# A planner that writes each engine's order: one plan in program order, against 25 plans ranked by latest starts

## The chip, the cores and the metric

The kernel runs on one core of a Trainium2 chip. A core has five engines that run their own instruction streams and meet only at semaphores: PE (TensorE, matrix products; its weight loads appear as PEld), DVE (VectorE), ACT (ScalarE), POOL (GpSimd) and SP (SyncE, which issues nearly all DMA transfers here). The metric is the device time of one execution in microseconds; less is better. All arithmetic is in 32-bit floats.

## The reference

The sequence has 2048 positions and 512 channels. Two layers alternate, A, B, A, B, each on a layer norm of x and added to x:

```python
L = 2 * S                                            # layer A
kv = k_shift * v                                     # k_shift: 4 taps, causal, per channel
y = irfft2(rfft2(pad(kv)) * rfft2(pad(ssm_k)))[:S]   # long convolution per channel
y = y + kv * ssm_D
A = q * y                                            # q = layernorm(x)

P = exp((A * dt)[:, :, None] * pos)                  # layer B: 128 modes per channel
K = 2.0 * einsum("dn,dnl->dl", C, P).real            # its convolution kernel, 512 x 2048
B = irfft(rfft(K) * rfft(u))[:L] + u * D_skip        # u = layernorm(x)
```

A's y does not depend on x, and B's K does not either, so each is computed once and used twice.

## The kernel before

The Fourier transforms are products with constant matrices on PE (w1, w2 forward, mm and w4 back). The channels are worked in four quarters of 128, each quarter in four groups of 32, and the frequencies in eight chunks.

The work has two parts, and the planner orders each as a whole.

Part 1 (2211 operations) holds two streams and the start of a third.

- The K stream makes B's kernel in 64 taps, four to each of 16 groups. A tap is: PE computes angles (pa, from tt and rw) and subtracts the whole turns (y on DVE, then pa<-y,minus on PE), ACT takes Abs and five Sin, POOL and DVE multiply by the magnitudes m (xy, and e on DVE), and PE contracts (pk<-xy,e; the number behind e names the tap). The magnitudes are Exp on ACT, for two groups at a time. After a group DVE writes ks, SP stores it (kdram) and loads it back (kk), PE and DVE transform it (pf<-kk, zk, pf<-zk), ACT copies the spectrum (pc) and SP stores it (spec). Exp and Sin need different ACT tables, and ordering edges in the program keep the Exp and Sin phases apart.
- The A stream forms kv (prod on POOL, kv<-prod,minus on PE, prod on DVE, stored in kv_d), the spectrum of ssm_k (through kk and zk as well), and then convolves quarter by quarter: u loaded from kv_d, pf<-u, transposes zu, pf<-zu, products vv and sw with the loaded spectrum kab on DVE, pf<-vv and pf<-sw, ACT copies zu, DVE transposes w, PE forms kv<-w, ACT copies and SP stores ya, and DVE updates the tile xq of the residual (two operations, kv<-kv,rs and xq<-kv,xq). When a quarter's four groups are done, SP stores xq in x1_d (shown as x_d), and xq, which has one buffer, is loaded for the next quarter; POOL subtracts a mean first.
- The start of the first B layer: x is loaded from x_d, a normalizer makes its scale rs and offset nb, and u, pf<-u and zu follow.

Part 2 (824 operations) is the first B convolution (pu<-zu, copies sw on ACT, products vv on DVE and sw on POOL, pi<-vv and pi<-sw, copies ie, transposes w, po<-w, x<-x,po, statistics st<-x), then the second A layer (`gated_update`: x is multiplied row block by row block by ut, made from the stored ya), a normalizer for each half of the rows, and the second B convolution, which ends in yo and its stores. Before the second convolution adds to x, `restore` on DVE adds the mean off back to each of 16 row blocks (x<-x,off). A restore of a row block has to follow the operations u that read the block.

Who sets the order: the helper `Planner` records every operation (`record`), and at `flush` it makes a plan and emits the instructions of each engine in the plan's order, with edges that keep this order. `cost` gives each operation how long it holds its engine and when its result is there. `plan` is a list scheduler in time: among the operations whose producers are planned it takes, again and again, the one that could begin earliest; where several could begin at the same time on an engine, the smaller rank goes first. The buffers that an operation needs have to be free, DMAs share eight lanes, large two-input products on DVE and POOL exclude each other, and the PE clock is taken as half after a little used window of 3413 ns. Before, rank is the place in the program, and there is one plan (`best`):

```python
    def best(self):
        return self.plan()
```

All instructions of the planned parts are issued from one line, 411 before and 485 in the changed kernel, so they are told apart by tiles. Line 178 (179) issues the prelude, which is not planned. In the profile pf stands for several PSUM tiles that share a pool.

Of the kernel before, what the change touches and what calls it, by code (L numbers as in the profile page):

```python
# [18 lines left out]
L, D, NM = 2048, 512, 128  # L19
# [88 lines left out]

class Planner:
    FIFO = False  # L110
    RELEASE = {"V": 34, "S": 60, "G": 90, "T": 80, "D": 27}

    def __init__(self, tc, nc):
# [107 lines left out]
    def prepare(self):  # L221
        ops = self.ops
        self.costs = [self.cost(op) for op in ops]
        for op in ops:
            op.before = {o for o in op.before if ops[o.n:o.n + 1] == [o]}
            op.ordered = [o for o in op.ordered if ops[o.n:o.n + 1] == [o]]
            op.late = [(o, lead) for o, lead in op.late if ops[o.n:o.n + 1] == [o]]
        self.follow = [[] for _ in ops]
        for op in ops:
            for o in op.before:  # L230
                self.follow[o.n].append((op.n, True))
            for o in op.ordered:
                self.follow[o.n].append((op.n, False))
            for o, lead in op.late:
                self.follow[o.n].append((op.n, lead))
        self.pending = [len(op.before) + len(op.ordered) + len(op.late) for op in ops]
        names, self.prior, self.queue = {}, [], {}
        self.using, self.users, self.gate, self.tag, self.handles, self.buffers = [], [], [], [], [], {}
        self.held = {p: [] for p in self.over.values()}
        for op in ops:  # L240
            l = []
            for t in op.uses:
                if t.tag_meta is None:
                    continue
                if t.name not in names:
                    names[t.name] = len(self.prior)
                    pool = next((p for p in self.over if f"_{p}_" in t.tag), None)
                    self.gate.append(self.over.get(pool))
                    q = self.queue.setdefault(t.tag, [])
                    ring = self.name(t) not in self.shared  # L250
                    self.prior.append(q[-t.tag_meta.bufs] if ring and len(q) >= t.tag_meta.bufs else None)
                    self.tag.append(None if ring else t.tag)
                    self.handles.append(t)
                    q.append(len(self.prior) - 1)
                    if not ring and len(q) <= t.tag_meta.bufs:
                        self.buffers.setdefault(t.tag, []).append(t)
                    self.users.append(0)
                l.append(names[t.name])
                self.users[names[t.name]] += 1
            self.using.append(l)  # L260
            for p, h in self.held.items():
                if any(f"_{p}_" in t.tag for t in op.uses if t.tag_meta is not None):
                    h.append(op.n)

    def plan(self, rank=None):
        ops, costs, prior, using = self.ops, self.costs, self.prior, self.using
        rank = rank or list(range(len(ops)))
        pending, left = list(self.pending), list(self.users)
        idle, live = [0.0] * len(prior), [False] * len(prior)
# [8 lines left out]
        ready = [0.0] * len(ops)  # L278
        start, end = [0.0] * len(ops), [0.0] * len(ops)
        avail = {e: [] for e in self.engines}  # L280
        lanes, server, lock = [0.0] * 8, 0.0, {"V": 0.0, "G": 0.0}
        act, window, clock = {}, 0, 0.5
        for op in ops:
            if not pending[op.n]:
                avail[op.engine].append(op.n)
        for waiting in range(len(ops)):
            best = None
            for e, l in avail.items():
                pick = None
                base = free[e]  # L290
                if e == "D":
                    base = max(base, min(lanes))
                for n in l:
                    t = max(base, ready[n])
                    if e in "VG" and costs[n][2]:
                        t = max(t, lock["G" if e == "V" else "V"])
                    if pick is not None and (t, rank[n]) >= pick[:2]:
                        continue
                    ok = True
                    for u in using[n]:  # L300
                        if live[u]:
                            continue
                        if self.gate[u]:
                            if rest[self.gate[u]]:
                                ok = False
                                break
                            t = max(t, last[self.gate[u]] + self.RELEASE[e])
                        tag = self.tag[u]
                        if tag:
                            if not open_[tag] or (self.FIFO and self.queue[tag][head[tag]] != u):  # L310
                                ok = False
                                break
                            t = max(t, min(spare[tag][b] for b in open_[tag]) + self.RELEASE[e])
                            continue
                        if prior[u] is None:
                            continue
                        if left[prior[u]]:
                            ok = False
                            break
                        t = max(t, idle[prior[u]] + self.RELEASE[e])  # L320
                    if not ok:
                        continue
                    if pick is None or (t, rank[n]) < pick[:2]:
                        pick = (t, rank[n], n)
                if pick is not None and (best is None or pick[0] < best[0]):
                    best = (pick[0], pick[2], e)
            if best is None:
                return None
            t, n, e = best
            op = ops[n]  # L330
            avail[e].remove(n)
            for u in using[n]:
                tag = self.tag[u]
                if tag and not live[u]:
                    fit = [b for b in open_[tag] if spare[tag][b] + self.RELEASE[e] <= t + 1e-6]
                    self.place[u] = max(fit, key=lambda b: (spare[tag][b], -b))
                    open_[tag].remove(self.place[u])
                    head[tag] += 1
                live[u] = True
            o, lat, extra = costs[n]  # L340
            start[n] = t
            if e == "T":
                k = int(t / 3413)
# [3 lines left out]
                o = o / clock  # L347
                a = extra * o / max(costs[n][0], 1e-9) * clock / 1.0
# [26 lines left out]
            for f, real in self.follow[n]:  # L375
                pending[f] -= 1
                ready[f] = max(ready[f], end[n] + self.RELEASE[ops[f].engine] if real is True else start[n] + o if real is False else end[n] - real)
                if not pending[f]:
                    avail[ops[f].engine].append(f)
        self.length = max(end)  # L380
        return sorted(range(len(ops)), key=lambda n: (start[n], n))

    def best(self):
        return self.plan()

    @staticmethod
    def name(t):
# [913 lines left out]
```

## Time and profile before

| | us |
|---|---|
| runs | 715.59, 710.18, 705.59 |
| median of the runs | 710.18 |
| the profiled execution | 708.18 |
| its span, first to last instruction | 706.2 |

The profiled execution is 2.0 us under the median and 2.0 us over its own span. A page of the profile gives busy time per engine; a view by windows gives the same for stretches of the span, with the TensorE clock that was granted there (1.00 is full speed); the chain of waits follows the work that ended last back from the end; a timeline lists instructions with the idle time ahead of them and what ended it. PE busy time is modelled from pipelined matmuls, so a busy PE is not PE at its peak.

### The profile page before, as it was taken

What the parts mean: (1) busy time and instruction counts of PE and PEld (TensorE: products, weight loads), DVE (VectorE), ACT (ScalarE), POOL (GpSimd) and SP (SyncE); (2) the same over time, 40 slices, a digit from 0 to 9 for tenths busy, and PEclk for the clock granted to TensorE, in tenths of its full rate; (3) what the DMA queues carried; (4) which work ended last, traced back from release to release, by engine and by line L of the source; (5) the groups of instructions that cost most, each with busy time, mean ns of one, the idle gap of its engine ahead of it and who ended that gap; (6) DMA issues with size and microseconds to landing.
All of it is one profiled execution on the core that took longest, in us unless ns stands there. A gap on an engine that the chain in (4) does not pass through costs nothing. (4 is left out here: it accounts for less than half of the span.)

```text
span 706.2 us, 20796 instructions
## 1 busy us (share of the span) xinstructions
PE 536.0 (76%) x8568; PEld 297.8 (42%) x8568; DVE 473.4 (67%) x900; ACT 405.4 (57%) x768; POOL 352.7 (50%) x344
## 2 busy tenths in 40 slices
PE   1398789899888876888887894527997832789984
PEld 0124334344344344554453562213664601356652
DVE  7345653456436571878899597555678889798783
ACT  3238566857597768776265763446653418837441
POOL 3739958969777362622252644103543510255561
PEclk9999998999998696999899898759999965999998
DMA  9699996876655253555786655786766421057884
GB/s 250 211 231 254 304 228 181 223 204 204 232 168 180 82 175 104 178 184 160 224 277 217 188 167 165 253 268 220 265 248 241 153 90 59 2 185 252 297 259 89
DMA packets 74499, 138.95 MB, mean 197 GB/s; under 512 B 8093, under 2 KB 37157, under 8 KB 72357
## 3 DMA queue, kind: packets, MB, share of 16 engines
q1 hardware_dynamic: 73540, 135.21, 63.1%
q0 software_dynamic: 864, 2.43, 1.0%
q8 instruction: 67, 1.10, 0.7%
q14 instruction: 28, 0.22, 0.1%
HBM read 97.75 MB, written 39.85 MB: 195 GB/s over the span
## 5 line engine op out<-in xcount | busy, mean ns | idle before, releaser
L411 POOL TENSOR_TENSOR xy<-tt,m 128x512 f32<-128x512 f32 x128 | 148.3, 1184 | 128.4 <-issue 73.6
L411 POOL TENSOR_TENSOR sw<-sw,kab 128x512 f32<-128x512 f32 x64 | 81.2, 1292 | 116.5 <-ACT sw L411 105.0
L411 POOL TENSOR_TENSOR prod<-kvt 128x512 f32<-128x512 f32 x64 | 79.9, 1274 | 7.5 <-DVE st L411 4.9
L411 PE MATMUL pf<-u,w 64*128 64x512 f32 (+1 forms) x200 | 60.1, 693 | 28.6 <-ACT u L411 15.9
L411 PE MATMUL kv<-prod,minus 128*128 128x512 f32 x128 | 75.9, 684 | 2.9 <-POOL prod L411 2.0
L411 DVE TENSOR_TENSOR e<-pa,m 128x512 f32<-128x512 f32 x64 | 43.4, 680 | 46.5 <-ACT pa L411 42.5
L411 PE MATMUL pf<-kk,w 64*128 64x512 f32 x128 | 45.7, 757 | 38.0 <-DMA kk<-ssmk_in 13.7
L411 ACT ACTIVATE m<-pf 128x1024 f32<-128x1024 f32 x48 | 47.7, 1024 | 44.0 <-PE pf L411 42.5
L411 DVE STREAM_TRANSPOSE zu<-pf 128x512 f32<-128x512 f32 x96 | 63.2, 692 | 12.4 <-PE pf L411 12.4
L411 DVE TENSOR_SCALAR y<-pa 128x512 fp32r<-128x512 f32 x64 | 43.5, 681 | 31.2 <-PE pa L411 29.2
L411 DVE STREAM_TRANSPOSE zk<-pf 128x512 f32<-128x512 f32 x64 | 42.0, 692 | 31.7 <-PE pf L411 31.7
L411 ACT ACTIVATE ab<-pa 128x512 f32<-128x512 f32 x64 | 38.2, 597 | 42.1 <-PE pa L411 42.0
L411 ACT COPY ie<-pi 128x1024 f32<-128x1024 f32 x32 | 32.3, 1010 | 52.1 <-PE pi L411 52.1
L411 DVE TENSOR_TENSOR vv<-pu,kab 128x512 f32<-128x512 f32 x64 | 42.8, 678 | 24.6 <-ACT sw L411 20.0
L411 PE MATMUL pi<-vv,mm 64*64 64x128 f32 x1024 | 53.7, 277 | 3.4 <-DVE vv L411 2.6
L411 PE MATMUL pi<-sw,mm 64*64 64x128 f32 x1024 | 52.4, 272 | 0.0
L411 ACT COPY sw<-pu 128x1024 f32<-128x1024 f32 x32 | 32.3, 1012 | 31.8 <-PE pu L411 22.4
L411 PE MATMUL pk<-xy,e 128*32 128x64 f32 x2048 | 45.7, 234 | 5.1 <-POOL xy L411 3.6
L411 ACT COPY pc<-pf 128x512 f32<-128x512 f32 x64 | 35.6, 585 | 22.9 <-DMA spec<-pc 13.8
L411 PEld LDWEIGHTS pk<-xy,e 128*32 128x32 f32 x2048 | 34.7, 117 | 31.7 <-issue 16.7
L411 PE MATMUL po<-w,w 128*64 128x512 f32 x128 | 36.8, 675 | 11.6 <-DVE w L411 11.5
L411 ACT ACTIVATE u<-x,nb,rs 128x128 f32<-128x128 f32 x101 | 40.8, 482 | 6.4 <-DMA x<-x_d 5.3
(121 smaller groups left out, 1083.9 us busy)
## 6 DMA issues: line engine op xcount, KB each, us to landing
kab<-spec SPq DMA_DIRECT2D x94, 512.0 KB, 4.8
spec<-pc SPq DMA_DIRECT2D x64, 256.0 KB, 3.4
kvt<-kv_in SPq DMA_DIRECT2D x32, 312.0 KB, 4.8
kk<-ssmk_in SPq DMA_DIRECT2D x32, 128.0 KB, 4.9
xr<-x_in SPq DMA_DIRECT2D x8, 512.0 KB, 8.6
kv_d<-prod SPq DMA_DIRECT2D x16, 256.0 KB, 3.3
kdram<-ks SPq DMA_DIRECT2D x64, 64.0 KB, 1.8
kk<-kdram SPq DMA_DIRECT2D x32, 128.0 KB, 2.6
```

The lines of the kernel that those rows point to most:

```text
L411: ins = getattr(self.engines[op.engine], name)(*a, **k).ins
```

## The change

The planner now plans 25 times for each part and keeps the shortest plan.

- The first plan has program order as its rank, as before, but amended costs: an activation whose table is not the loaded one begins `SWAP` = 1290 ns after its engine is free, and an operation that has to wait for more than one other engine pays `EXTRA` per further engine (37 ns on DVE, 60 on ACT, 54 on POOL, 90 on PE).
- `latest` goes back through a plan from its end: over data edges, over the order in which buffers were handed on, and gives each operation the latest start that would not lengthen the plan.
- In 24 turns the rank is made from these latest starts of the turn before (turns 0, 3, 6, ...: the latest start alone; 1, 4, ...: latest plus actual start; 2, 5, ...: the place in order of the latest starts plus the place in the program).
- A new condition, `need`, keeps an operation from taking a shared buffer while an unshared buffer that its user needs is not free yet, so that a plan with other ranks cannot lock itself.

In part 1 the order of turn 3 is kept, in part 2 that of turn 6; both rank by the latest start alone. The instructions are the same in kind and number on every engine, and there are 21 ACT_TABLE_LOAD before and after.

```diff
+    SWAP, EXTRA = 1290, {"V": 37, "S": 60, "G": 54, "T": 90, "D": 0}
...
+        groups = {"Sin": "Sin", "Exp": "Exp", "Sqrt": "Sqrt", "Ln": "Ln", "Arctan": "Arctan"}
+        self.table = [groups.get(getattr(op.calls[0][1][2], "name", None)) if op.calls[0][0] == "activation" else None
+                      for op in ops]
+        self.sources = [[o.n for o in op.before] for op in ops]
...
+        self.need = [set() for _ in self.prior]
+        for l in self.using:
+            for u in l:
+                if self.tag[u]:
+                    self.need[u].update(w for w in l if not self.tag[w])
+        self.need = [{w for w in s if self.prior[w] is not None and self.prior[w] not in s} for s in self.need]
...
-                    t = max(base, ready[n])
+                    t = max(base + (self.SWAP if self.table[n] not in (None, table) else 0), ready[n])
...
+                            if any(not live[w] and left[prior[w]] for w in self.need[u]):
+                                ok = False
+                                break
...
+            table = self.table[n] or table
+            waits = set()
+            for m in self.sources[n]:
+                if ops[m].engine != e and start[m] > seen.get((e, ops[m].engine), -1.0):
+                    waits.add(ops[m].engine)
...
+            t += self.EXTRA[e] * max(0, len(waits) - 1)
...
+    def latest(self):
...
+        late = [0.0] * len(ops)
+        for a in sorted(range(len(ops)), key=lambda n: (-start[n], -n)):
+            late[a] = min([late[f] - lag for f, lag in after[a]], default=self.length) if after[a] else self.length
+            late[a] = min(late[a], self.length - (end[a] - start[a]))
+        return late
+
+    TURNS = 24
+
     def best(self):
-        return self.plan()
+        order = self.plan()
+        best = self.length, order, self.place, self.starts, self.ends
+        for turn in range(self.TURNS):
+            late, early = self.latest(), self.starts
+            if turn % 3 == 2:
+                place = sorted(range(len(late)), key=lambda n: late[n])
+                rank = [0.0] * len(late)
+                for i, n in enumerate(place):
+                    rank[n] = i + n
+            else:
+                rank = [l + (e if turn % 3 else l) for l, e in zip(late, early)]
+            order = self.plan(rank)
+            if order is None:
+                break
+            if self.length < best[0]:
+                best = self.length, order, self.place, self.starts, self.ends
+        self.length, order, self.place, self.starts, self.ends = best
+        return order
```

Three places where instructions stand otherwise are shown with the prediction's steps.

More of the change, by code (lines that the diff above doesn't have):

```diff
@@ L282, in plan @@
         act, window, clock = {}, 0, 0.5
+        table, seen = None, {}
         for op in ops:
@@ L340, in plan @@
             o, lat, extra = costs[n]
+            table = self.table[n] or table
[3 more added lines that the diff above has]
+                    waits.add(ops[m].engine)
+            for m in self.sources[n]:
+                key = e, ops[m].engine
+                seen[key] = max(seen.get(key, -1.0), start[m])
+            t += self.EXTRA[e] * max(0, len(waits) - 1)
             start[n] = t
@@ L379, in plan @@
                     avail[ops[f].engine].append(f)
-        self.length = max(end)
+        self.length, self.starts, self.ends = max(end), start, end
         return sorted(range(len(ops)), key=lambda n: (start[n], n))
-    def best(self):
-        return self.plan()
+    def latest(self):
+        ops, start, end = self.ops, self.starts, self.ends
+        after = [[] for _ in ops]
+        for a in range(len(ops)):
+            for f, real in self.follow[a]:
+                lag = end[a] - start[a] + self.RELEASE[ops[f].engine] if real is True else (
+                    self.costs[a][0] if real is False else end[a] - start[a] - real)
+                after[a].append((f, lag))
+        first, users, chains, pairs = {}, {}, {}, []
+        for a in sorted(range(len(ops)), key=lambda n: start[n]):
+            for u in self.using[a]:
+                first.setdefault(u, a)
+                users.setdefault(u, []).append(a)
+        for u in first:
+            if self.tag[u]:
+                chain = chains.setdefault((self.tag[u], self.place[u]), [])
+                if chain:
+                    pairs.append((chain[-1], u))
+                chain.append(u)
+            elif self.prior[u] in users:
+                pairs.append((self.prior[u], u))
+        for p, u in pairs:
+            for a in users[p]:
+                after[a].append((first[u], end[a] - start[a] + self.RELEASE[ops[first[u]].engine]))
+        late = [0.0] * len(ops)
[3 more added lines that the diff above has]
+        return late
```

## The prediction

> **What bounds the kernel now.** I read the page's busy times, then a view by windows cut where the kind of work changes, then the chain of waits and timelines of the stretches in which no engine is full. First the page: PE is busiest, at 76%, so no engine bounds the whole.
>
> ```profile
> span 706.2 us, 20796 instructions
> PE 536.0 (76%) x8568; PEld 297.8 (42%) x8568; DVE 473.4 (67%) x900; ACT 405.4 (57%) x768; POOL 352.7 (50%) x344
> ```
>
> The windows are: the start; K taps beside A's kv; K taps beside A's convolution; end of part 1 and x's reload; first B convolution; second gated update; last B convolution.
>
> ```profile
> core 0: us, PE busy (x) PEld busy (x) DVE busy (x) ACT busy (x) POOL busy (x), PEclk, DMA share, GB/s
> 0.00:44.00 44.00, 16.03 (x28) 4.43 (x28) 23.00 (x36) 11.36 (x17) 21.41 (x35) 0.96 0.86 229
> 44.00:220.00 176.00, 156.79 (x1869) 74.00 (x1869) 90.03 (x158) 121.14 (x252) 143.27 (x136) 0.96 0.79 222
> 220.00:425.00 205.00, 168.12 (x3070) 101.50 (x3068) 150.93 (x263) 137.97 (x271) 86.70 (x84) 0.88 0.58 177
> 425.00:480.00 55.00, 24.93 (x300) 11.30 (x302) 34.53 (x97) 24.97 (x57) 10.13 (x11) 0.72 0.75 236
> 480.00:560.00 80.00, 67.19 (x1496) 44.90 (x1491) 59.66 (x108) 39.91 (x57) 40.22 (x32) 0.98 0.66 234
> 560.00:620.00 60.00, 30.46 (x288) 14.32 (x278) 50.68 (x151) 32.72 (x70) 9.84 (x15) 0.74 0.13 45
> 620.00:706.20 86.20, 72.52 (x1549) 47.35 (x1544) 64.60 (x90) 37.37 (x48) 41.17 (x33) 0.95 0.71 222
> ```
>
> Both B convolutions keep PE at .84. The second row has PE at .89 and POOL at .81 while DVE has half its time free; the third has PE at .82 with a clock of .88, DVE at .74 and POOL at .42. So in the bulk the mix is uneven, and the fourth and sixth rows are chains in which PE is half idle. There is the time that an order can move.
>
> **The change, part by part.** It adds and removes no instruction; all its price is in order. The first tap of A's convolution on PE:
>
> ```profile
> L411 PE MATMUL pf<-u,w x200: 376/664/1219, 220.3 to 666.4; 64*128 64x512 f32 x92, 64*128 64x256 f32 x8
> ```
>
> On PE, where A's convolution begins (pf<-u), before; pk<-xy,e ends a K tap:
>
> ```order
> L411 MATMUL pk<-xy,e_622 32x64 x16
> L411 MATMUL pa<-y,minus 128x512
> L411 MATMUL pf<-kk,w_107 128x16x16x2 x2
> L411 MATMUL pa<-y,minus 128x512
> L411 MATMUL pf<-kk,w_107 128x16x16x2 x2
> L411 MATMUL pa<-tt,rw 128x512
> L411 MATMUL pf<-u,w_107 128x16x16x2 x2
> ```
>
> The same place on PE in the changed kernel:
>
> ```order
> L485 MATMUL pk<-xy,e_574 32x64 x16
> L485 MATMUL kv<-prod,minus 128x512
> L485 MATMUL pf<-zk,w_108 64x128 x16
> L485 MATMUL kv<-prod,minus 128x512
> L485 MATMUL pa<-y,minus 128x512
> L485 MATMUL pf<-u,w_107 128x16x16x2 x2
> ```
>
> The convolution moved from behind tap 29 (e_622) to behind tap 24 (e_574), and it runs beside kv products that POOL feeds.
>
> *Bulk, 44 to 425.* DVE-heavy work enters a stage where DVE is half free, and POOL-heavy taps are left for the stage where POOL has 58% free. PE's share over both stages is (156.79+168.12)/381 = .853. If the evener mix brings the second stage to that share it lasts 168.12/.853 = 197.1 instead of 205: **−7.9, taken**. Best end: it reaches the first stage's .891, 188.7, −16.3. Worst end: the more interleaved work leaves longer gaps, as in the slice 240 to 280, with 30.30/40 = .757: 222.1, +17.1. I take −7.9 as the value between the two measured stages, the nearest rows of such a mix.
>
> ```profile
> 160.00:200.00 40.00, 35.96 (x429) 16.95 (x429) 19.64 (x31) 25.81 (x51) 32.84 (x31) 1.00 0.65 205
> 240.00:280.00 40.00, 30.30 (x520) 18.90 (x524) 21.43 (x38) 28.99 (x61) 18.19 (x20) 0.76 0.46 140
> ```
>
> At the head SP issues the first rw loads behind 21 other transfers instead of 9, and POOL's kv products start later, but PE has the spectrum work (pf<-kk, pf<-zk) in their place; I cost that at nothing, and if that cover fails it falls within the range above.
>
> *End of part 1.* Of the windows' fourth row, 425.22 to 457.56 lies between the stores of the third and fourth residual quarter (x_d<-xq), 32.3 us. The chain:
>
> ```profile
> 425.22 0.34 SPq L411 DMA_DIRECT2D x_d<-xq  x1
> 429.76 1.25 SPq L411 DMA_DIRECT2D xq<-x_in  x2
> 433.36 2.13 SPq L411 DMA_DIRECT2D xq<-x_in  x2
> 436.89 1.79 SPq L411 DMA_DIRECT2D kdram<-ks  x4
> 438.96 4.03 POOL L411 TENSOR_TENSOR xq<-xq,off 128x512 f32<-128x512 f32 x4 [4.88 <-DMA xq<-x_in]
> 440.17 1.19 SPq L411 DMA_DIRECT2D kk<-kdram  x2
> 443.03 0.69 DVE L411 SCALAR_TENSOR_TENSOR xq<-kv,xq 128x512 f32<-128x512 f32 x1 [5.64 <-POOL xq L411]
> 443.69 2.16 PE L411 MATMUL pf<-kk,w 64*128 64x512 f32 x4 [8.18 <-DMA kk<-kdram]
> 445.78 1.97 PE L411 MATMUL kv<-w,w 128*64 128x512 f32 x4
> 445.89 1.31 DVE L411 STREAM_TRANSPOSE zk<-pf 128x512 f32<-128x512 f32 x2 [2.17 <-PE pf L411]
> 447.68 2.34 PE L411 MATMUL pf<-zk,w 64*64 64x128 f32 x64
> 450.51 1.08 PE L411 MATMUL kv<-w,w 128*64 128x512 f32 x4 [0.48 <-DVE xq L411]
> 457.56 0.32 SPq L411 DMA_DIRECT2D x_d<-xq  x1
> 440.77 2.78 DMA kk<-kdram
> ```
>
> The last K taps still run after the store; their kernel goes through kdram, and A's second kv<-w stands behind pf<-kk on PE, which waits 8.18 for the load. On PE the end of part 1, before:
>
> ```order
> L411 MATMUL pk<-xy,e_1082 32x64 x16
> L411 MATMUL pf<-kk,w_107 128x16x16x2 x2
> L411 MATMUL pk<-xy,e_1093 32x64 x16
> L411 MATMUL pf<-kk,w_107 128x16x16x2 x2
> L411 MATMUL kv<-w,w_110 64x512 x2
> L411 MATMUL pf<-zk,w_108 64x128 x32
> L411 MATMUL kv<-w,w_110 64x512 x2
> L411 MATMUL pf<-zk,w_108 64x128 x32
> L411 MATMUL kv<-w,w_110 64x512 x2
> ```
>
> And in the changed kernel:
>
> ```order
> L485 MATMUL pf<-vv,mm 64x128 x4
> L485 MATMUL pf<-sw,mm 64x128 x4
> L485 MATMUL pf<-kk,w_107 128x16x16x2 x2
> L485 MATMUL kv<-w,w_110 64x512 x2
> L485 MATMUL pf<-kk,w_107 128x16x16x2 x2
> L485 MATMUL pf<-zk,w_108 64x128 x64
> L485 MATMUL kv<-w,w_110 64x512 x6
> ```
>
> All taps (e_1093 is the last) now stand ahead of A's last products, and the whole transform of the last kernel ahead of kv<-w of the groups 1 to 3. On SP, kdram is issued behind the third store and ahead of xq's loads, kk's last pair between the two pairs of xq. Counting from the store: the first pair of xq can go at +4.5 as before (429.76−425.22), kk's pair 1.19 and the second xq pair 1.25 behind it, so +8.2; landed 438.96−433.36−2.13 = 3.5 later, +11.7; POOL's four subtractions 4.03, +15.8 (before +17.8). The K side: kk issued by +7.0, landed 2.78 later, +9.8; pf<-kk 2.16, zk 1.31, and 64 pf<-zk twice 2.34: +18.0. Then come kv<-w of the groups 1 to 3; the first of them before stood at 445.78−425.22 = 20.6. So −2.5, and the pf<-zk that stood between two kv<-w are gone and the first kv<-w runs at 1.08 instead of 1.97, −0.9: **−3.4**. Ends: 0, if SP's loads are as late as before, and −4.8, if K's side is entirely covered (15.8 against 20.6).
>
> *Second gated update.* DVE is 84% busy from 560 to 620, and here its order counts:
>
> ```profile
> 603.78 0.17 DVE L411 TENSOR_TENSOR nb<-nm,rs 128x8 f32<-128x8 f32 x1
> 603.98 1.70 DVE L411 TENSOR_SCALAR u<-x,rs,nb 128x128 f32<-128x128 f32 x6
> 605.73 1.99 PE L411 MATMUL pf<-u,w 64*128 64x256 f32 x12 [0.36 <-POOL u L411]
> 608.35 1.73 DVE L411 TENSOR_SCALAR x<-x,off 128x512 f32<-128x512 f32 x4 [2.67 <-ACT u L411]
> 610.00 4.90 DVE L411 STREAM_TRANSPOSE zu<-pf 128x512 f32<-128x512 f32 x8
> 611.46 3.27 PE L411 MATMUL pf<-u,w 64*128 64x512 f32 x8 [3.74 <-DVE zu L411]
> ```
>
> DVE waits 2.67 for ACT's u to restore x (x<-x,off), and the transposes zu, for which PE then waits 3.74, are queued behind that. On DVE at this place, before:
>
> ```order
> L411 TENSOR_SCALAR u<-x,rs,nb 128x128 x6
> L411 TENSOR_SCALAR x<-x,off 128x512 x4
> L411 STREAM_TRANSPOSE zu<-pf 128x512 x8
> L411 TENSOR_SCALAR x<-x,off 128x512
> L411 STREAM_TRANSPOSE zu<-pf 128x512 x2
> ```
>
> And in the changed kernel:
>
> ```order
> L485 TENSOR_SCALAR u<-x,rs,nb 128x128 x6
> L485 TENSOR_TENSOR nb<-nm,rs 128x8
> L485 TENSOR_SCALAR u<-x,rs,nb 128x128 x5
> L485 STREAM_TRANSPOSE zu<-pf 128x512 x10
> L485 TENSOR_SCALAR x<-x,off 128x512
> ```
>
> The restores moved behind the transposes, into the last convolution, where DVE is .75 and PE .84 busy and which therefore covers them. But five more u stand on DVE, since the first half's normalizer and u now come only behind the last rows. Five u of 1.70/6 = .28 are 1.4, so zu can begin about 1.4 behind the 605.7 at which u ends, near 607.0 instead of 610.0: **−3.0**. Ends: 0, if the late first half makes PE's first pf<-u as late as the restores made zu, and −4.3, if zu comes at 605.7.
>
> *The rest.* In the first B convolution some statistics move behind transposes of w, with PE at .84 as the bound; last tail unchanged: 0, ±2.
>
> ACT's table loads are now charged. Their price in the trace:
>
> ```profile
> L411 ACT ACT_TABLE_LOAD x17 | 21.8, 1283 | 6.0 <-DVE zk L411 3.6 <-DVE zu L411 2.2
> 389.78 1.03 ACT m L411
> 390.83 1.28 ACT L411
> 392.12 1.05 ACT tt L411 x3
> ```
>
> One load takes 1.28, and Sin starts right behind it; the planner's 1290 is that. The Trainium skill, ScalarE: Activation LUTs, section What ACT_TABLE_LOAD costs, adds a drain of about 1.38 us to each load; by that page the plan would still be 17 × 1.38 = 23 us of ACT time short (an estimate), but these rows show no such drain.
>
> **Sum.** 708.2 − 7.9 − 3.4 − 3.0 = 693.9, so **694.0**. The profiled execution is 2.0 under the median of 710.18, and the runs spread by ±5.
>
> **Rivals.**
> 1. *The bulk gives nothing.* Its gaps come from chains across engines, not from the mix; for it speaks that POOL's .81 in the first stage already leaves PE .89. Then 708.2 − 3.4 − 3.0 = 701.8. That the ranks do nothing of what they say is ruled out by the listings, except in the bulk, where it is this case.
> 2. *The interleaving thins PE and the clock falls.* For it: a slice that mixes both streams already ran with PE at .757 and a clock of .76, while the slice 160 to 200, with .90, had 1.00. If the second stage falls to .757, the bulk costs 17.1 and the time is 718.9; 725.3 if both tails also give nothing. It decides below a PE share of 168.12/(205+6.4) = .795, where the tails' gains are used up. Against it: even in the sixth window, with PE at 30.46/60 = .51, the clock was still .74, and DVE, ACT and POOL have room in both stages. The Trainium skill, TensorE: Matmul & The Clock Gate, section What's actually happening, says that the clock goes to half after an idle window of some 3.4 us, so longer single gaps would cost more than their length; the two slices agree in direction, and by that rule this rival would be somewhat dearer than its price here.
> 3. *The mix evens out wholly.* The second stage reaches .891: 708.2 − 16.3 − 6.4 = 685.5. Against it: DVE at .74 would have to go to .80 on average.
>
> **Chances.** The forecast's case (687 to 699) .45, rival 1 .20, rival 2 .15, rival 3 .17, others .03. A measurement of this kernel can tell about 2% from no change: 696.0 and 724.4. Faster: two thirds of the forecast's case and rival 3, with a little of the others, .49. Slower: those of rival 2 with the tails lost and some of the others, .09. Same: .42. The range goes from 680.0 (708.2 − 16.3 − 4.8 − 4.3 − 2 = 680.8) to 722.0, between rival 2's two times; a tenth is left out above, some hundredths below.
>
> **What would show it.** Bulk: the first pf<-u clearly ahead of 220, and from 44 to the third x_d<-xq less than 381 with PE's share above .853 and a clock above .88. End of part 1: the third to the fourth x_d<-xq under 32.3, and kv<-w of groups 1 to 3 in one row, not behind a wait for kk. Update: no restore between u and zu on DVE, zu some 3 from the last nb (6.2 before). Wrong if: pf<-u is early but POOL's taps then run out late; the last xq loads are stuck on SP behind spectrum stores; or zu waits for PE.

## The result and the profile after

| | before | changed |
|---|---|---|
| median of the runs, us | 709.21 (4 runs, 705.59 to 715.59) | 679.54 (4 runs, 674.84 to 683.90) |
| the profiled execution | 708.18 | 683.90 |
| its span | 706.2 | 681.4 |

The ratio is 0.9571, with a 95% interval from 0.947 to 0.9673: faster by 3.3 to 5.3%. The forecast of 694.0 had the direction; the time lies just under its range. The changed kernel's profiled execution is 4.4 over its median, so the stretches below add up to 24.8 us, less than the 29.7 between the medians.

The page of the changed kernel, its first lines:

```profile
span 681.4 us, 20786 instructions
PE 529.9 (78%) x8568; PEld 294.5 (43%) x8568; DVE 474.3 (70%) x900; ACT 407.0 (60%) x768; POOL 353.1 (52%) x344
```

Work is the same; PE, DVE and ACT have it packed closer. The view by windows of the changed kernel, cut at events: first transforms; to the third store x_d<-xq; to the fourth; to the first pu of the first B convolution; to the first ut; to the last convolution's first pu; end.

```profile
core 0: us, PE busy (x) PEld busy (x) DVE busy (x) ACT busy (x) POOL busy (x), PEclk, DMA share, GB/s
0.00:39.50 39.50, 9.89 (x20) 2.90 (x20) 21.58 (x35) 11.36 (x17) 12.79 (x27) 1.00 0.80 218
39.50:403.83 364.33, 326.64 (x4888) 171.65 (x4892) 245.63 (x424) 263.96 (x530) 242.03 (x229) 0.94 0.73 210
403.83:446.30 42.47, 21.59 (x320) 11.62 (x312) 19.95 (x40) 10.52 (x17) 7.49 (x10) 0.74 0.59 165
446.30:467.20 20.90, 5.73 (x16) 1.82 (x17) 13.64 (x55) 10.62 (x28) 0.00 (x0) 0.61 0.89 271
467.20:563.80 96.60, 74.73 (x1648) 49.54 (x1648) 77.69 (x172) 44.15 (x66) 43.15 (x35) 0.97 0.62 216
563.80:591.66 27.86, 15.61 (x44) 7.60 (x45) 25.80 (x74) 25.46 (x59) 4.36 (x10) 0.73 0.11 38
591.66:681.40 89.74, 75.71 (x1644) 49.35 (x1644) 69.98 (x102) 40.91 (x55) 43.30 (x34) 0.96 0.68 213
```

The same cut of the kernel before, for the bulk and for the first B convolution:

```profile
44.00:425.22 381.22, 325.14 (x4940) 175.57 (x4944) 241.18 (x422) 259.33 (x521) 229.97 (x219) 0.91 0.68 198
479.20:583.47 104.27, 79.24 (x1648) 50.43 (x1648) 78.28 (x172) 44.12 (x65) 42.98 (x35) 0.93 0.56 198
```

In the bulk PE was idle for 381.2 − 325.1 = 56.1 us and is so for 37.7 now; its share went from .853 to .897. Cut once more at the first pf<-u (220.3 and 200.5), it went from .89 to .92 ahead of A's convolution and from .82 to .88 beside it. PE's three longest waits in the bulk before, each ended by work of the K stream (m, e, y), and the same three now, by the view of waits (us in total, times, longest):

```profile
PE pf L411 <- ACT m L411: 10.1, 10, 1.9
PE pa L411 <- DVE e L411: 8.7, 12, 2.9
PE pa L411 <- DVE y L411: 5.3, 10, 1.4
```

```profile
PE pf L485 <- ACT m L485: 5.7, 11, 1.5
PE pa L485 <- DVE e L485: 5.7, 10, 1.1
PE pa L485 <- DVE y L485: 2.4, 4, 0.8
```

Not all waits shrank: PE's wait for the products vv of A rose from 1.6 to 5.2. From the start times of the same events in both traces (nb is the last one on DVE):

| stretch | before | changed | difference | forecast |
|---|---|---|---|---|
| start to third x_d store | 425.22 | 403.83 | −21.4 | −7.9 |
| third to fourth x_d store | 32.34 | 42.47 | +10.1 | −3.4 |
| to the first pu | 21.60 | 20.90 | −0.7 | 0 |
| first pu to first ut (first B convolution) | 104.30 | 96.56 | −7.7 | 0 |
| first ut to last nb | 20.31 | 19.74 | −0.6 | 0 |
| last nb to first pu of the last convolution | 11.26 | 8.15 | −3.1 | −3.0 |
| from there to the end | 91.19 | 89.74 | −1.4 | 0 |

Three terms are off: the bulk gained more than twice what was said, the end of part 1 lost instead of gaining, and the first B convolution gained where nothing was expected.

### The profile page after: what moved, and what is told of

Its sections match the earlier page's. It is cut to its first block, busy times and chain, and to the rows that moved or that the text cites. A ratio compares the mean times of both kernels' runs of the same rounds, so it can differ in the third digit from the quotient of the medians.

```text
span 681.4 us, 20786 instructions
## 1 busy us (share of the span) xinstructions
PE 529.9 (78%) x8568; PEld 294.5 (43%) x8568; DVE 474.3 (70%) x900; ACT 407.0 (60%) x768; POOL 353.1 (52%) x344
## 5 line engine op out<-in xcount | busy, mean ns | idle before, releaser
L485 PE MATMUL pf<-u,w 64*128 64x512 f32 (+1 forms) x200 | 56.8, 659 | 22.8 <-ACT u L485 19.2
L485 ACT COPY pc<-pf 128x512 f32<-128x512 f32 x64 | 35.4, 588 | 59.8 <-PE pf L485 42.0
L485 ACT COPY ie<-pi 128x1024 f32<-128x1024 f32 x32 | 32.3, 1009 | 49.2 <-PE pi L485 49.2
L485 ACT ACTIVATE m<-pf 128x1024 f32<-128x1024 f32 x48 | 47.1, 1027 | 16.3 <-PE pf L485 15.2
L485 ACT COPY sw<-pu 128x1024 f32<-128x1024 f32 x32 | 32.1, 1012 | 24.2 <-PE pu L485 13.6
L485 PE MATMUL pf<-zk,w 64*64 64x128 f32 x1024 | 39.0, 295 | 6.4 <-DVE zk L485 4.6
```

What stands on the lines that cost most here:

```text
L485: ins = getattr(self.engines[op.engine], name)(*a, **k).ins
```

## The experiments

Each was timed beside the kernel before on the same chip; the medians of the kernel before lay between 710.0 and 711.5 there. The times are medians, the ratio is to the kernel before.

| run | us | ratio (95%) |
|---|---|---|
| e1_costs_only | 696.83 | 0.9789 (0.9738 to 0.9839) |
| e2_turns_only | 708.36 | 0.9940 (0.9900 to 0.9979) |
| e3_part1_new | 693.00 | 0.9722 (0.9655 to 0.9788) |
| e4_part2_new | 695.99 | 0.9786 (0.9726 to 0.9846) |
| e5_ya_first | 672.40 | 0.9475 (0.9417 to 0.9534) |
| e6_shift_only | 720.11 | 1.0164 (1.0092 to 1.0237) |
| e7_swap_only | 691.00 | 0.9734 (0.9662 to 0.9806) |
| e8_swap_2660 | 686.15 | 0.9669 (0.9603 to 0.9736) |
| e9_stats_late | 702.10 | 0.9799 (0.9718 to 0.9880) |
| e10_restore_late | 709.11 | 0.9953 (0.9915 to 0.9990) |
| e11_charges_low | 675.43 | 0.9460 (0.9378 to 0.9542) |
| e12_charges_high | 679.42 | 0.9519 (0.9454 to 0.9583) |
| e13_random_ranks | 700.12 | 0.9887 (0.9833 to 0.9941) |
| e14_first_turn | 696.28 | 0.9781 (0.9702 to 0.9860) |

**Charges and turns apart.**

```diff
-    TURNS = 24
+    TURNS = 0
```

> The changed planner with no turns: one plan in program order, with the charges for table loads and second waits. Its order begins A's convolution behind the same tap as the changed kernel (e_574, before e_622). Theory (the early start evens the mix in the bulk): nearly the whole bulk gain of 17 to 21 us stays and the time is 685 to 693. Rival (the ranking by latest start makes the gain, the charges do nothing alone): within 4 us of the kernel before, 705 to 713.

```diff
-    SWAP, EXTRA = 1290, {"V": 37, "S": 60, "G": 54, "T": 90, "D": 0}
+    SWAP, EXTRA = 0, {"V": 0, "S": 0, "G": 0, "T": 0, "D": 0}
```

> 24 turns with ranks from latest starts, but no charge for table loads and none for second waits. A's convolution begins behind e_545, earlier still. Theory (early start): the bulk gain stays, 677 to 690. Rival (the charges are what makes the plan fit the chip): the plan misjudges ACT and the time is 700 to 712.

For the charges neither theory holds whole; for the turns alone the rival came. The charges alone give 13.5 us (710.4 to 696.8), the turns alone 2.0, both together 29.7: one needs the other. PE's idle time from the start to the third x_d store says the same: 84.1 us before, 75.2 with the charges alone, 86.2 with the turns alone, 67.3 with both. Charges alone begin A's convolution at 194.3, earlier than the changed kernel (200.5), and yet reach the third x_d store only at 414.4. The reason why the turns alone bring so little is in ACT's groups, of e2:

```profile
L485 ACT ACT_TABLE_LOAD x27 | 34.6, 1283 | 0.5
L485 ACT ACTIVATE m<-pf 128x1024 f32<-128x1024 f32 x48 | 47.4, 1031 | 10.7 <-PE pf L485 10.3
```

There are ten loads more than the 17 before, 12.8 us of ACT. A timeline of e2's ACT shows them: Exp (m) and Sin (tt and pa) take turns, each with its load.

```profile
63.95 0.67 ACT L485 ACTIVATE tt<-pa 128x256 f32<-128x256 f32 x2
64.64 1.28 ACT L485 ACT_TABLE_LOAD   x1
65.93 1.94 ACT L485 ACTIVATE m<-pf 128x1024 f32<-128x1024 f32 x2
67.89 1.28 ACT L485 ACT_TABLE_LOAD   x1
69.19 0.48 ACT L485 ACTIVATE pa<-ab,halfpi 128x256 f32<-128x256 f32 x1
...
71.92 1.28 ACT L485 ACT_TABLE_LOAD   x1
73.22 1.02 ACT L485 ACTIVATE m<-pf 128x1024 f32<-128x1024 f32 x1
74.26 1.28 ACT L485 ACT_TABLE_LOAD   x1
```

Ranked by how late each could begin, with loads free, Exp for a later group slips in between the Sin of an earlier one. In e7 below the charge for loads alone prevents that. The same groups of the changed kernel, and m of the kernel before:

```profile
L485 ACT ACT_TABLE_LOAD x17 | 21.8, 1283 | 0.4 <-DVE zk L485 0.2
L485 ACT ACTIVATE m<-pf 128x1024 f32<-128x1024 f32 x48 | 47.1, 1027 | 16.3 <-PE pf L485 15.2 <-POOL prod L485 0.5 <-DMA rw<-rows_d 0.5
```

```profile
L411 ACT ACTIVATE m<-pf 128x1024 f32<-128x1024 f32 x48 | 47.7, 1024 | 44.0 <-PE pf L411 42.5 <-POOL xy L411 0.7 <-DMA rw<-rows_d 0.5
```

The column behind the second bar is ACT's idle time ahead of Exp. Before, ACT sat 44.0 us ahead of its 48 Exp, nearly all of it waiting for PE's products; now 16.3, with no load more. This wait by itself is no measure of the gain: it is 50.1 with the charges alone, which gained, and 10.7 with the turns alone, which hardly did.

**The parts apart.** The changed planner for one part, the old one for the other (no charges, no turns):

```diff
     def prepare(self):
+        self.part = getattr(self, "part", 0) + 1
+        old = self.part in self.OLD
+        self.TURNS, self.SWAP = (0, 0) if old else (24, 1290)
...
```

> The new order in part 1 alone; part 2 as before. If the parts add, as the two traces say (part 2 with 7.7 in the first B convolution, 3.7 in the second update and 1.4 in the last convolution), 679.5 + 12.8 = 692.3. Rival (what part 2 gained came from another state of the clock or of the DMAs behind part 1, not from its own order): 680 to 685.

> The new order in part 2 alone; part 1 as before. If the parts add, 709.2 - 12.8 = 696.4. Rival (part 2 gains only behind the new part 1): 704 to 710.

The parts add: 692.3 and 696.4 were expected, 693.0 and 696.0 came. So part 2 gained by its own order. In e4 the first B convolution takes 97.2, near the changed kernel's 96.6, behind an old part 1.

**The early start alone.**

```diff
     def best(self):
-        return self.plan()
+        return self.plan([op.n + op.shift for op in self.ops])
```

Here shift is 200 for what the K stream records and 0 for the rest.

> The kernel before with its old planner, no charges and no turns; only the ranks of the K stream's operations are made 200 places later, which begins A's convolution behind e_574 as in the changed kernel. Theory (the early start evens the mix): most of what the charges alone gave comes back, 694 to 699. Rival (where A begins is only a sign, and the gain is in finer order): 705 to 712.

The kernel became slower by 0.9 to 2.4%, which neither named. The taps of the K stream (pk), first and last start, before, in e6 and in the changed kernel:

```profile
L411 PE MATMUL pk<-xy,e x2048: 216/219/317, 57.9 to 435.3; 128*32 128x64 f32 x187
```

```profile
L412 PE MATMUL pk<-xy,e x2048: 217/219/317, 92.0 to 456.4; 128*32 128x64 f32 x187
```

```profile
L485 PE MATMUL pk<-xy,e x2048: 216/219/317, 70.7 to 407.2; 128*32 128x64 f32 x187
```

And e6's window from the third x_d store to the first pu:

```profile
406.01:486.24 80.23, 47.16 (x523) 22.64 (x522) 43.52 (x112) 46.26 (x99) 25.05 (x26) 0.66 0.56 170
```

In e6 A's convolution is done as early as in the changed kernel (fourth x_d store at 446.3 in both), but K's taps end 21 us later than before, so what A won is paid back in a stretch, third store to first pu, of 80.2 us with PE at .59. PE's idle time up to the third store is 363.3 − 307.7 = 55.6, as before (56.1). In the changed kernel A and K both end earlier. So an early start does not suffice. The edit is not the early start alone, for it holds back the whole K stream (first tap at 92.0 instead of 57.9), but other runs agree: e2 begins A's convolution at 206.2 and PE idles as before up to the third store, and e7 below begins it at 210.7 and idles 69.2, near the changed kernel's 67.3.

**Which charge, and how exact.**

```diff
-    SWAP, EXTRA = 1290, {"V": 37, "S": 60, "G": 54, "T": 90, "D": 0}
+    SWAP, EXTRA = 1290, {"V": 0, "S": 0, "G": 0, "T": 0, "D": 0}
```

> 24 turns and the charge of 1290 ns for a table load, no charge for second waits. Theory (without the charge for loads the latest starts mix Exp and Sin, 27 planned loads instead of 17, and that ate the gain of the turns): 17 loads again and 677 to 686. Rival (the charges for second waits count as much): 690 to 702.

The same line with SWAP at 2660 is e8, with 1250 and 33, 54, 49, 81 e11, with 1320 and 40, 65, 58, 97 e12.

> As the changed kernel, with 2660 ns for a table load instead of 1290, the price with the drain that the Trainium skill gives (ScalarE: Activation LUTs, What ACT_TABLE_LOAD costs). Theory (the load costs 1.28 us and nothing beside it, as the trace shows): no better than the changed kernel, 678 to 690. Rival (the drain is real and the plan with 1290 is late on ACT): better by some 4 us or more, under 675.

> The changed kernel with charges a little lower: 1250 ns for a load, 33, 54, 49 and 81 ns for second waits on DVE, ACT, POOL and PE. The plan that is kept comes out another one. Theory (with loads charged, the 25 plans are near each other in worth, and which is kept is a matter of some us): 17 planned loads and 676 to 694. Rival (the charges are met exactly by the change, and a tenth off spoils the plan): over 696.

> The changed kernel with charges a little higher: 1320 ns for a load, 40, 65, 58 and 97 ns for second waits. Theory as for the lower charges: 17 planned loads and 676 to 694. Rival: over 696.

The charge for loads turns e2's 27 loads into 17 and gives 17 us of the median; PE's idle time from 43.9, where the bulk begins, to the third x_d store is 37.1 with it, as in the changed kernel (37.7). But 691.0 lies in the rival's range. Of the remaining 11 us the traces put most into part 2 (222.0 from the first pu to the end in e7, 214.2 in the changed kernel). That this is the second waits' worth is not shown: e11 and e12 begin A's convolution at 188 and 177, e12 has 19 loads where 17 were expected, and with orders so unlike they come out at 675 and 679. Four sets with both charges lie between 675 and 686, so a change of the charges by itself can move the time by that much. e8, with the price that the Trainium skill states for a load (ScalarE: Activation LUTs, What ACT_TABLE_LOAD costs: 1283 ns and a drain of 1380), gained nothing over 1290, and each load in the rows above is followed at once by its Exp; here the drain is not seen.

**Ranks or choice.** Random ranks in place of latest starts, with the same choice of the shortest of 25; and the first ranked plan without a choice:

```diff
...
+            noise = np.random.RandomState(turn).randn(len(self.ops))
+            rank = [n + 10 * r for n, r in enumerate(noise)]
...
```

> The changed planner with its charges and 24 turns, but each turn's rank is the place in the program plus a random number (normal, 10 places wide) instead of the latest starts; the shortest of the 25 plans is kept. Theory (the ranks by latest start are what the turns bring): no better than the charges alone, 692 to 702. Rival (any 24 further plans to choose from would do): 675 to 688.

```diff
-    TURNS = 24
+    TURNS = 1
...
-            if self.length < best[0]:
+            if True:
```

> The changed planner with its charges, and of its turns only the first, kept whatever its length: the rank is the latest start in the plan in program order. Theory (the rank does it, the choice among many adds little): 678 to 690. Rival (the choice among 25 plans does it): 694 to 704.

Random ranks of this kind, near the program's order, do no better than the charges alone (700.1 against 696.8), so a choice among 25 plans is not enough by itself. The first ranked plan fell into the rival's range, against the theory: at 696.3 its median is nearly that of the charges alone, 696.8. So one ranking by latest starts is not enough either, and no run of e14 (688.6 to 699.0) comes down to those of the changed kernel (674.8 to 683.9). The later rankings, the choice, or both make the difference; which of them stays open, and only one plan of one ranking was run.

The traces show less than the medians, because e14's profiled execution is 7.7 under its median and the changed kernel's 4.4 over: 686.8 against 681.4. In them e14 is 13.6 ahead at the fourth x_d store (432.7 against 446.3) and loses that and 2.3 more up to the first pu, for which it takes 36.8 instead of 20.9.

**The new wait at the end of part 1.** On ACT the last four copies pc of the spectrum stand behind the three last copies ya of A, and on SP the last four spectrum stores behind the last x_d store; the rest is the changed kernel's plan.

```diff
-        for n in order:
+        for n in self.hand(order):
```

> The changed kernel's plan with one edit by hand at the end of part 1: on ACT the last three copies ya stand ahead of the last four spectrum copies pc, and on SP the last four spectrum stores stand behind the last x_d store. Theory (ya waits on ACT behind pc copies that wait for spectrum stores to land, and with it the last quarter's chain): from the third to the fourth x_d store 42.5 becomes 33 to 36 and the whole time falls by 6 to 9 us against the changed kernel, to 671 to 674. Rival (the chain is late for its loads and the DMAs, the copies are only what is seen): under 2 us, 678 to 681.

The changed kernel's timeline at the place, a bracket being the idle time ahead and what ended it:

```profile
423.87 11.80 SPq L485 DMA_DIRECT2D spec<-pc  x8
427.19 1.09 PE L485 MATMUL kv<-w,w 128*64 128x512 f32 x4
428.80 0.58 ACT L485 COPY pc<-pf 128x512 f32<-128x512 f32 x1 [2.13 <-DMA spec<-pc]
433.64 0.58 ACT L485 COPY pc<-pf 128x512 f32<-128x512 f32 x1 [4.26 <-DMA spec<-pc]
435.22 0.59 ACT L485 COPY ya<-kv 128x512 f32<-128x512 f32 x1
435.85 0.70 DVE L485 TENSOR_TENSOR kv<-kv,rs 128x512 f32<-128x512 f32 x1 [6.28 <-ACT ya L485]
437.42 1.97 PE L485 MATMUL kv<-w,w 128*64 128x512 f32 x4 [9.14 <-DVE xq L485]
```

And of e5:

```profile
428.76 1.08 PE L500 MATMUL kv<-w,w 128*64 128x512 f32 x4
429.89 0.58 ACT L500 COPY ya<-kv 128x512 f32<-128x512 f32 x1 [2.58 <-PE kv L500]
432.60 1.08 PE L500 MATMUL kv<-w,w 128*64 128x512 f32 x4 [2.76 <-DVE xq L500]
438.97 2.06 ACT L500 COPY pc<-pf 128x512 f32<-128x512 f32 x4
```

In the changed kernel kv is done at 428.3, but ya waits on ACT behind copies pc, which wait for spectrum stores to free their buffers; PE's next kv<-w starts 10.2 us after the first. In e5 it starts 3.8 after. The stretch went from 42.5 to 35.4, as expected, and the time to 672.4. (The profiled execution of e5 is 7.4 over its median, so the stretch is compared here, not the span.) This beats both kernels; its interval overlaps that of the changed kernel, so that it beats that one rests on the 7.1 us of the stretch.

The stretch is still 3.0 longer than before (32.3). From the first kv<-w of the groups 1 to 3 to the fourth store it takes 11.8 in e5, as in the kernel before, and 19.1 in the changed kernel; so the edit takes away what ACT's order cost. What is left lies ahead of that kv<-w, which starts 23.6 after the third store in e5, 23.4 in the changed kernel and 20.6 before. There the last pair of kk is issued 9.4 after the third store, and PE gets it 14.1 after it:

```profile
417.91 1.89 PE L485 MATMUL pf<-kk,w 64*128 64x512 f32 x4 [3.25 <-DMA kk<-kdram]
```

**Part 2: statistics and restores.** In the kernel before, the statistics st on DVE in part 2 get a rank 40 places later.

```diff
+                if name == "bn_stats" and "st_" in a[0].tensor.name + "_":
+                    rank[op.n] += 40
```

> The kernel before with its old planner; only the statistics st on DVE in part 2 get a rank 40 places later, so that transposes and products go ahead of them in the first B convolution. Theory (there the statistics stood ahead of transposes for which PE waited): from the first pu to the first ut 104.3 becomes 97 to 100, the whole 703 to 707. Rival (the stage is bound by PE, the order of DVE is hidden): 103 to 105 and 709 to 712.

The first B convolution took 99.8 instead of 104.3, so this order alone brings 4.5 of the 7.7; the whole came out a little lower than expected, at 702.1 with runs from 694.7 to 705.2. The piece where most is won: two of PE's rows of the kernel before, with their waits, then the window around them before, and the window of the same piece (from the third quarter's first pu to the fourth quarter's) in the changed kernel:

```profile
530.85 1.13 PE L411 MATMUL pf<-u,w 64*128 64x512 f32 x4 [1.69 <-DVE zu L411]
541.62 1.09 PE L411 MATMUL po<-w,w 128*64 128x512 f32 x4 [2.16 <-DVE w L411]
```

```profile
520.20:544.50 24.30, 19.50 (x420) 12.50 (x420) 19.09 (x39) 7.72 (x8) 10.01 (x8) 1.00 0.62 217
```

```profile
508.00:526.50 18.50, 17.63 (x410) 12.20 (x412) 13.71 (x21) 7.26 (x8) 10.08 (x8) 1.00 0.63 215
```

PE's idle time there went from 4.8 to 0.9. DVE had 19.1 us of work in the piece and has 13.7 now; of the difference some 2.9 are statistics (16 before, 2 now), the rest a transpose of w, two of zu and an addition to x. Cut exactly from pu to pu, the piece takes 23.7 before, 18.5 in the changed kernel and 19.7 in e9, where PE's idle time is 0.9 too. So 4.1 of e9's 4.5 are won here. Over the whole stage PE's idle time fell by 3.2 and its busy time by 4.5 (79.2 to 74.7) at a clock of .93 and then .97; how far the higher clock is a gain of its own was not taken apart.

In the kernel before, the restores ahead of the first ten zu of the last convolution were put behind them by hand, as a block:

```diff
+        order = [n for n in order if n not in move]
+        at = order.index(turns[-1]) + 1
+        return order[:at] + move + order[at:]
```

> The kernel before with one edit by hand: on DVE the restores that stood ahead of the first ten transposes zu of the last convolution stand behind them. Theory (the prediction's term for the second update): from the last nb to the second convolution's first pu 11.3 becomes 8.0 to 9.0, the whole falls by 2 to 3 us, 706 to 708 beside 709 to 711 of the kernel before; the stretch behind is as long as before. Rival (the restores only move the wait): the stretch from first pu to the end grows by as much.

Both were partly right. From the last nb to the first pu it took 7.7 instead of 11.3, but the stretch to the end grew from 91.2 to 94.0. The two together are worth 0.7; the median fell by 2.4 (by the interval, 0.1 to 0.9%).

```profile
609.10 2.82 DVE L426 TENSOR_SCALAR x<-x,off 128x512 f32<-128x512 f32 x7
611.84 1.27 DVE L426 TENSOR_TENSOR vv<-pu,kab 128x512 f32<-128x512 f32 x2
613.26 1.11 PE L426 MATMUL pu<-zu,w 64*64 64x128 f32 x32 [2.09 <-DVE vv L426]
```

Seven restores in a row now hold up vv, for which PE waits. The changed kernel puts them between other work in smaller lots (1, 1, 2, 2, 5 and so on) and keeps the gain (89.7 to the end).

## Why the prediction was right and wrong

- *Bulk, −7.9, measured −21.4.* The direction was right, the size and the cause wrong. The step that failed is "If the evener mix brings the second stage to that share": the early start was taken for the cause, and the two stages' shares for the bounds. e6 begins A behind the same tap with no less idle time of PE, and e2 and e7 begin it within 4.5 us of each other with 86.2 and 69.2 us of idle time. The shares were no bounds: the first stage, which the sum left at .89, rose to .92, and the second passed .853 to reach .88. What came in its place is an order in which PE waits less, above all for the K stream: its idle time fell by 18.4, its waits for m, e and y from 24.1 to 13.8. By e1, e2 and e7 this takes the ranks and a charge for loads together; which moves in the order do it was not isolated. Rival 3 had nearly the size for the bulk (−16.3 for a share of .891; .897 came, and 364.3 instead of 381.2), though from the same wrong cause. The cut at 44 and 39.5 puts 4.5 of the 21.4 at the head, which had been costed at nothing.
- *End of part 1, −3.4, measured +10.1.* Two steps failed. The working followed PE, POOL and SP's loads, and left ACT out. The rows of the forecast's listing showed pf<-zk of the whole last kernel ahead of kv<-w; each such product ends in copies pc on ACT and stores on SP, which count as moved too. The wait named as removed (for kk) shrank from 8.18 to 3.25, and a wait of 9.14 took its place. e5 shows it: the stretch falls by 7.1 once ya is not behind pc. The other step is the K side of the sum, +18.0 to the first kv<-w: it came at +23.4, because kk's last pair was issued at +9.4 instead of +7.0 and reached PE at +14.1 instead of +9.8. This is 5.4 of the miss of 13.5, and e5 does not remove it.
- *Second update, −3.0, measured −3.1.* Right, by the mechanism named: no restore stands between u and zu, and zu begins 2.6 from the last nb instead of 6.2. e10 bears on what the step had taken for granted, that the last convolution covers the restores: seven in a row it does not cover. The rows of nb and zu in the changed kernel:

```profile
583.51 0.28 DVE L485 TENSOR_TENSOR nb<-nm,rs 128x8 f32<-128x8 f32 x1
586.10 1.32 DVE L485 STREAM_TRANSPOSE zu<-pf 128x512 f32<-128x512 f32 x2 [0.83 <-PE pf L485]
```

- *The rest, 0, measured −7.7 in the first B convolution.* "With PE at .84 as the bound" was the failing step: .84 is an average over stretches in which PE is full and stretches in which it waits for DVE. The waits of 1.69 and 2.16 stood in the trace. e9 shows that the order of the statistics brings 4.5 of it; the remainder of some 3 us was not taken apart.
- *Rival 2,* that interleaving thins PE and lowers the clock, did not come: the clock rose from .91 to .94 in the bulk. e6 ran its stretch from the third store to the first pu at a clock of .66, but there K's taps run out late behind A's; that is no case of interleaving, so whether interleaving can lower the clock is not shown.
- *The charge for loads* was written off as a matter of price. e2 and e7 show that it counts for where the loads are put: without it there are 27.
- *Luck.* The bulk and the end of part 1 missed by 13.5 each, in opposite directions, so that these two errors cancel. The terms put at 0 and −3.0 make up the 10.5 us by which the traces gained more than forecast (24.8 against 14.3).

## What to carry to other kernels

A planner's charge works together with its ranks: latest starts gained 2 us without charges and the charges 13.5 without latest starts, 29.7 together, so try them crossed before judging either. By the medians a single ranking added nothing to the charges; the gain came with the 24 turns and the choice among them. When an order is moved, follow each moved product to its last consumer on every engine, the copies and stores too; the greater part of the miss at the end of part 1 sat on the one engine that was left out. An average busy share is no bound: look for the waits inside the stage, and do not take one visible shift (an earlier start) for the cause before it was tried alone.

## What was not expected

A few per cent up to a tenth on the charges give quite other orders (A's convolution begins at 188, 201 or 177) at 675 to 680 us, so within that the exact charge hardly mattered here. And spectrum stores that go out in a row hold their four buffers long: in the changed kernel ACT waited 2.13 and then 4.26 for a store to land before it could copy again, and SP, which had to wait for those copies in turn, took 11.80 us over eight stores. In e5, where four stand there, ya followed at once.
